# Sigmoid attention and a ReGLU layer in one kernel: a third unit of seven products in batch 2, whole chunks between the units, bursts of five and three

## The chip, the cores and the metric

One core of one Trainium2 chip runs the whole kernel in one launch. The time is the device time of one execution in microseconds. The engines are TensorE (PE; PEld is its weight load), VectorE (DVE), ScalarE (ACT), GpSimd (POOL) and SyncE (SP). POOL issues the loads, SP the DMA transposes and most stores.

## What is computed

```python
# q, k, v: (8 batches, 12 heads, 448 tokens, 64), float32
scores = q @ k.T / sqrt(64) - log(448)
attn = sigmoid(scores)
x = (attn @ v)  # heads side by side: 3584 tokens x 768
gate = maximum(x @ w_gate, 0)      # w_gate, w_val: 768 x 1536
val = x @ w_val
out = (gate * val) @ w_out         # w_out: 1536 x 768
```

## The kernel before

The kernel works in float16 with sums in float32 and goes over the batches 0 to 7. In each batch, scores are made in 21 *score units* (`qk_unit`): three groups `g` of four heads, seven query chunks `c` each; the order is g = 0 for units 0 to 6, g = 1 for 7 to 13, g = 2 for 14 to 20. A unit fills two PSUM banks and ScalarE takes the sigmoid of both into a tile PT. When a group's seven units are done, `pv` multiplies PT with v into two banks, and VectorE copies them, scaled, into `xT` (line 184). `pv` of a batch's last group (`pv_finish`) comes in the first burst of the next batch.

Scores come in *bursts* (`burst`), and between two bursts PE does work of the feed-forward layer of earlier batches. The order is written by hand: `cuts` splits the 21 units, `pv_at` puts the `pv`, `mix`, `hooks` and `given` say what goes between the bursts of batch 1, and `work` is the queue from batch 2 on. Within a burst the engines follow the order in which the program was written; each engine runs its own instructions strictly in that order.

The layer's 1536 columns are twelve *chunks* of 128. There are three forms of the work on them. A plain chunk (`gv`) is two products of six matmuls, a relu on ScalarE or VectorE, and a multiplication on VectorE into `hT`. For batch 0 chunks are done for 256 and 192 tokens apart (`HALVES`, `push_first`), in batch 1's mix. For batch 1, eight of twelve chunks are done as two *units of seven products* (`gv_split`, kind "s" in `work`): a seven-product block scheme, with four chunks and half the tokens at a time, that needs sums of weights (`gate_sums`, which overwrites part of `wv`, and S2, S1, S4 of `unit_sum_steps`) and of tokens (`split_sums`: T1, T2, T4, T3). The four other chunks of batch 1 are plain ("u"). From batches 2 and 3 on, pairs of batches use units "w" (`gv_pair`). The output is made in pairs of token tiles (`down_pair`, kind "y"), also with seven products; it needs sums of `wo` (`weight_sums(0..3)`, tiles T) and of `hT` (`token_sum_steps`). A pair in `SUMS_LATE` takes its products in another order, in which those that need no sums come first. In odd batches from 3 on, a burst lies inside a pair (`inner`, `amid`).

Within a unit or a pair, `ahead` is written before its first product, and `jobs` (`beside`) after the first few.

The eight PSUM banks are handed out in turn (`bank`, `later`), so a matmul that starts in a bank waits until the bank's last reader is done. SBUF tiles are shared in the same way by their tags.

From batch 2 on, q and k are turned around by `dma_transposes(b, g)`: two copies re-lay k and q of the group into a tile `rel` (VectorE, line 222), and one DMA transpose, issued by SP (line 226), writes `qkT`, which the group's score units read. `hold(b, g)` (line 857) is a copy on POOL that reads a `qkT`, so that the loads behind it on POOL's queue wait for the transpose. Batches 0 and 1 are transposed by PE.

The loads on POOL's queue are, in order: batch 0, weights w_gate and w_val in pieces, batch 1 between them, k and q of batch 2; then the hold for (2, 1), v of batch 2, batch 3, `wo`, and v of batch 3. The tiles of k and q of batches 0, 2, 3 and so on are one buffer, so a batch's load waits for the re-laying copies of the batch before.

Of the kernel before, what the change touches and what calls it, by code (L numbers as in the profile page):

```python
# [18 lines left out]
def kernel(  # L19
# [39 lines left out]
    gsbp = ctx.enter_context(tc.tile_pool(name="gsbp", bufs=6))  # L59
    first_sbuf = ExitStack()  # L60
# [34 lines left out]
    def tiles_of(b):  # L95
        if b not in in_tiles:
            pool = early if b == 1 else inp
# [59 lines left out]
    load_gv(6, 9)  # L157
    load_v(1)
    load(1, 2, 3, "kq")
    load_gv(9, 12)  # L160
# [57 lines left out]
    def dma_transposes(b, g):  # L218
        k16, q16, _ = in_tiles[b]
        rel = relp.tile([P, TW, P], FP16, tag="rel", name="rel")  # L220
        for ti, t16 in enumerate((k16, q16)):
            nc.vector.tensor_copy(  # L222
# [5 lines left out]
        )  # L228

# [136 lines left out]
    def open_late():  # L366
# [5 lines left out]
        late["X"] = pool.tile([P, 3, HD, S], FP16, tag="X", name="X")  # L372
        late["sums"] = ctx.enter_context(tc.tile_pool(name="sums", bufs=2))

# [28 lines left out]
    SUMS_LATE = {(1, 0), (1, 1), (2, 0), (2, 1), (3, NPP)}  # L403
# [152 lines left out]
    def early_sum_steps(j, f):  # L556
        views = []
        for i in range(3 * j, 3 * j + 3):
            t = early.tile([P, 2, 512], FP16, tag=f"PT{i}", name="S")
            flat = t[:].rearrange("p a y -> p (a y)")[:, 0 : HD * 2 * P]  # L560
            views.append(flat.rearrange("p (x y) -> p x y", y=2 * P))
# [15 lines left out]
    def batch_blocks(g, ks):  # L577
        x1, x2 = xT_tiles[2 * g], xT_tiles[2 * g + 1]
        lo, hi = slice(*ks), slice(HD + ks[0], HD + ks[1])
        return [late["X"][:, i, lo] for i in range(3)] + [x1[:, lo], x1[:, hi], x2[:, lo], x2[:, hi]]  # L580
# [13 lines left out]
    def gv_pair(g, f, beside, first_copy):  # L594
        x1, x2 = xT_tiles[2 * g], xT_tiles[2 * g + 1]
        T1, T2, T4 = (late["X"][:, i] for i in range(3))
# [77 lines left out]
    def split_sums(b):  # L674
        tile_ = xTp.tile([P, NPAIR, S], FP16, tag="xT", name="X2")
# [7 lines left out]
        sub(T1, B12, B11)  # L683
        sub(T2, B22, T1)
        sub(T4, B21, T2)
        sub(T3, B22, B12)
# [169 lines left out]
    def hold(b, g):  # L856
        nc.gpsimd.tensor_copy(gate[0:1, :], qkT_tiles[(b, g)][0:1, 0, 0:2])
# [40 lines left out]
    def next_work(jobs=(), alone=False, amid=None, ahead=()):  # L898
# [11 lines left out]
        if kind == "y":  # L910
            down_pair(g, i, beside, prepare, not work, scaled_act if alone else scaled, amid)
# [12 lines left out]
    for b in range(1, B):  # L924
        if b == 1:
            cuts, pv_at = (0, 3, 6, 9, 13, 17, 21), {3: (0, 2), 5: (1, 2)}
        else:
            cuts, pv_at = (0, 4, 7, 11, 14, 18, 21), {0: (-1, 2), 2: (0, 2), 4: (1, 2)}
# [8 lines left out]
        if b == 1:  # L937
            mix = (4, 3, 3, 3, 3, 4)
            hooks = {
                1: [(3, lambda: both(1, 1))],  # L940
                3: [(3, lambda: both(1, 2))],
                4: [(2, lambda: dma_transposes(2, 0)), (0, lambda: dma_transposes(2, 1))],
                5: [(4, late_loads)],
            }
            steps = itertools.chain.from_iterable(early_sum_steps(j, 2 * j) for j in range(4))
            given = ((0, 0, 1, 1, 1), (0, 1, 1, 1), (0, 1, 1, 1), (0, 1, 1, 0), (2, 0, 0, 0), (0, 1, 1, 1, 0))
# [15 lines left out]

        for m in range(count):
# [4 lines left out]
            if b == 2 and m == 3:  # L968
                jobs += [lambda: dma_transposes(3, 0), lambda: dma_transposes(3, 1)]
            elif b == 3 and m == count - 1:  # L970
# [6 lines left out]
            if b == 1:  # L977
                if m == 0:
                    load(2, 0, 1, "kq")
                    load(2, 1, 2, "kq")  # L980
                    load(2, 2, 3, "kq")
            elif m == (2 if b == 4 else 0) and b + 1 < B:
# [3 lines left out]
            if b == 2 and m == 0:  # L986
# [69 lines left out]
```

## Time and profile before

| | |
|---|---|
| median of 3 runs | 388.48 us (388.12 to 389.19) |
| the profiled execution | 389.02 us |
| its span, first to last instruction | 387.2 us |
| granted clock of TensorE, mean | 0.998 |
| batch 1's bursts and what lies between | 29.00 to 61.29 us |
| batch 2's | 61.29 to 95.79 us |
| the first output pair with its two bursts, in batch 3 | 95.79 to 105.73 us |
| issue of the transposes (2, 0), (2, 1), (2, 2) | 53.62, 56.10, 59.08 us |
| issue of the transposes (3, 0), (3, 1), (3, 2) | 82.64, 87.28, 96.04 us |
| POOL's hold passes | 60.16 us |
| v of batch 3, the last load behind it, landed | 92.16 us |

The times inside the execution are counted from the first instruction. Busy time of an engine is time in which it executes an instruction; a matmul's end is modelled, and matmuls that follow each other overlap in the table of groups. The time before a landing includes waiting in the queue.

### The profile page before, as it was taken

Reading aid. Unit: us, or ns where it says so; the run is one execution under the profiler, and the core shown is the slowest. Engines: PE = TensorE matmul, PEld = TensorE weight load, DVE = VectorE, ACT = ScalarE, POOL = GpSimd, SP = SyncE. Lnnn points to the kernel's source line nnn. Section 1 sums busy time; section 2 is a strip of 40 time slices with the busy share of each in tenths; the row PEclk is TensorE's granted clock in tenths of the full one; section 3 lists DMA queues with packets and bytes.
Section 4 is the critical chain, followed back from the end, with each engine's and each line's share of the span. In section 5 each row is a group of like instructions: output and inputs, shape, how many; then the busy total and the mean of one; then the engine's idle time right before and its main releaser. Section 6 shows DMA issues by size and latency. Waiting matters only on the chain.

```text
span 387.2 us, 8977 instructions
## 1 busy us (share of the span) xinstructions
PE 381.0 (98%) x3570; PEld 223.2 (58%) x3570; DVE 304.5 (79%) x609; ACT 227.3 (59%) x480; POOL 49.9 (13%) x73
## 2 busy tenths in 40 slices
PE   8999999999999999999999999999999999999995
PEld 6678776885555545555555554545455555555563
DVE  3455667769868999999868789999978788999563
ACT  5967887567777645555777764545477344333321
POOL 9543306100400003000300300000000000000000
PEclk9999999999999999999999999999999999999999
DMA  9999999999969303952599893222012220000335
GB/s 169 199 199 204 204 194 163 208 208 130 182 150 193 81 2 40 184 90 47 44 228 224 164 231 60 48 50 50 0 38 72 71 69 0 2 0 0 83 88 159
DMA packets 67421, 43.81 MB, mean 113 GB/s; under 512 B 35634, under 2 KB 64050, under 8 KB 67378
## 3 DMA queue, kind: packets, MB, share of 16 engines
q0 software_dynamic: 28960, 23.24, 39.3%
q1 hardware_dynamic: 37634, 19.24, 24.4%
q10 hardware_dynamic: 784, 0.75, 0.6%
q8 instruction: 28, 0.46, 0.5%
q14 instruction: 15, 0.12, 0.1%
HBM read 47.19 MB, written 11.01 MB: 150 GB/s over the span
## 4 chain that ended last, share of the span: by engine, by line
PE 97%; ACT 2%; DVE 0%; issue 0%
PE u L385 35%; PE g L385 16%; PE y L385 12%; PE qk_ps L239 10%; PE pv_ps L257 8%; PE g_ps L322 5%; PE v_ps L322 5%; PE u L708 2%; PE g L708 2%; ACT PT L187 2%; PE warm_ps L175 1%; PE trt L204 1%; ACT ysb L446 0%; DVE ysb L540 0%; DVE zeros L130 0%
## 5 line engine op out<-in xcount | busy, mean ns | idle before, releaser
L187 ACT ACTIVATE PT<-qk_ps 128x448 f16<-128x448 f32 (+3 forms) x318 | 150.9, 584 | 79.7 <-PE qk_ps L239 79.5
L385 PEld LDWEIGHTS <-S 128*128 128x128 f16 x576 | 56.4, 98 | 45.9
L624 DVE TENSOR_TENSOR gsb<-g,gsb 128x448 f32<-128x448 f32 x72 | 42.8, 624 | 8.0 <-PE g L385 7.7
L239 PE MATMUL qk_ps<-qkT 64*64 64x448 f16 (+2 forms) x756 | 47.5, 337 | 1.0 <-ACT ysb L446 0.6
L385 PEld LDWEIGHTS <-hT 128*128 128x128 f16 x318 | 29.5, 98 | 24.0 <-issue 6.1
L257 PE MATMUL pv_ps<-PT,v 64*64 64x448 f16 (+2 forms) x756 | 36.6, 329 | 0.0
L464 DVE SCALAR_TENSOR_TENSOR ysb<-y,ysb 128x384 f32<-128x384 f32 x33 | 18.4, 556 | 21.3 <-PE y L385 14.3
L184 DVE TENSOR_SCALAR xT<-pv_ps 128x448 f16<-128x448 f32 (+2 forms) x53 | 27.8, 567 | 8.2 <-PE pv_ps L257 7.1
L385 PEld LDWEIGHTS <-wg 128*128 128x128 f16 x216 | 20.1, 98 | 21.8 <-issue 4.3
L385 PEld LDWEIGHTS <-wv 128*128 128x128 f16 x216 | 21.1, 98 | 19.7
L446 ACT ACTIVATE ysb<-u 128x384 f32<-128x384 f32 x28 | 13.8, 491 | 30.6 <-PE u L385 26.5
L239 PEld LDWEIGHTS <-qkT 64*64 64x64 f16 x756 | 17.7, 106 | 21.3 <-issue 14.2
L385 PE MATMUL u<-wo,hT 128*128 128x384 f16 x156 | 29.8, 327 | 0.0
L111 POOL DMA_DIRECT2D k<-in_k_dram x14 | 10.9, 776 | 142.0 <-DVE rel L222 136.3
L257 PEld LDWEIGHTS <-v 64*64 64x64 f16 x756 | 21.4, 107 | 11.1 <-issue 0.5
L385 PE MATMUL u<-xT,wg 128*128 128x448 f16 x108 | 23.5, 354 | 0.0
L385 PE MATMUL u<-X,S 128*128 128x448 f16 x108 | 23.4, 352 | 0.0
L385 PE MATMUL g<-xT,wg 128*128 128x448 f16 x108 | 23.4, 352 | 0.0
L385 PE MATMUL u<-X,wv 128*128 128x448 f16 x108 | 23.4, 352 | 0.0
L385 PE MATMUL g<-X,S 128*128 128x448 f16 x108 | 23.4, 352 | 0.0
L385 PE MATMUL g<-xT,S 128*128 128x448 f16 x108 | 23.4, 352 | 0.0
L385 PE MATMUL u<-xT,wv 128*128 128x448 f16 x108 | 23.4, 352 | 0.0
(98 smaller groups left out, 563.1 us busy)
## 6 DMA issues: line engine op xcount, KB each, us to landing
out_dram<-ysb SPq DMA_DIRECT2D x50, 192.0 KB, 3.9
v<-in_v_dram POOLq DMA_DIRECT2D x8, 336.0 KB, 15.3
v<-in_v_dram POOLq DMA_DIRECT2D x16, 168.0 KB, 15.2
k<-in_k_dram POOLq DMA_DIRECT2D x4, 672.0 KB, 12.0
q<-in_q_dram POOLq DMA_DIRECT2D x4, 672.0 KB, 15.0
wo<-in_moe_w_out_dram POOLq DMA_DIRECT2D x2, 1152.0 KB, 19.2
k<-in_k_dram POOLq DMA_DIRECT2D x9, 224.0 KB, 12.1
q<-in_q_dram POOLq DMA_DIRECT2D x7, 224.0 KB, 12.4
```

The costliest lines, as they stand in the source:

```text
L111: nc.gpsimd.dma_start(t16[:, xs, cs], rows_of(src, b)[:, xs, cs])
L175: nc.tensor.matmul(ps[:, 0:n], zeros[:, 0:P], zeros[:, 0:n], start=True, stop=True)
L184: nc.vector.tensor_scalar(out=xT, in0=src, scalar1=XSCALE, scalar2=None, op0=AOP.mult)
L187: nc.scalar.activation(PT_ap, ps_ap, AF.Sigmoid, bias=sig_bias, scale=qk_scale)
L239: nc.tensor.matmul(out_of(hh)[o : o + 64, :], qkT[rows, c, cols], qkT[rows, NCH + c0 : NCH + c1, cols], start=True, stop=True, tile_positi ...
L257: nc.tensor.matmul(ps[hh][64 * r : 64 * r + 64, 0:qn], v16[rows, 2 * g + hh, c * D : (c + 1) * D], pieces[c][rows, hh, :], start=(c == 0), ...
L322: nc.tensor.matmul(ps[:, 0:qn], (wg, wv)[i][:, dc, f * P : (f + 1) * P], xT_tiles[b][:, dc, q0 : q0 + qn], start=(dc == 0), stop=(dc == ND ...
L385: nc.tensor.matmul(ps[:, 0:n], A[:, k_, :], W[:, k_, :], start=(first and k_ == 0), stop=(k_ == kn - 1), skip_group_check=True,)
L446: nc.scalar.activation(o, ps[:, 0:HM], AF.Copy, scale=OUT_SCALE)
L464: nc.vector.scalar_tensor_tensor(out=o, in0=ps[:, 0:HM], scalar=OUT_SCALE, in1=o, op0=AOP.mult, op1=AOP.add)
L624: nc.vector.tensor_tensor(out=gs[u][i][:], in0=ps[u][:, 0:S], in1=gs[u][i][:], op=AOP.add)
L708: nc.tensor.matmul(ps[j // 2][:, j % 2 * SQ : (j % 2 + 1) * SQ], sets[j][i][:, k_, :], W[:, k_, :], start=(first and j % 2 == 0 and k_ == ...
```

## The change

- **Batch 1's chunks 8 to 11** become a third unit of seven products, `("s", 1, 8)`. Its sums are put into output tiles (`output_views`), step by step beside batch 2's work.
- **Batch 0's chunks 10 and 11** leave batch 1's mix and come in batch 2 as plain chunks of all 448 tokens, `("u", 0, 10)` and `("u", 0, 11)`. Batch 1 has 16 pieces between its bursts and not 20. The queue of batch 2 is s0, u10, s4, u11, s8, where it was u8, s0, u9, s4, u10, u11.
- **Bursts in batch 2**: five, of 5, 3, 5, 3 and 5 units, where there were six of 4 and 3.
- **Relus** of six pieces of batch 0, not two, are on VectorE.
- **Re-laying copies**: those of (3, 0) and (3, 1) are on ScalarE, in the second and third unit of batch 2. (2, 1) and T1 are written ahead of batch 2's first burst, (2, 2) beside the first unit, (3, 2) last beside the first output pair of batch 3.
- **Loads**: v of batch 1 earlier; weight chunks 9, then 10 and 11, later; a hold for the transpose of (2, 0), and behind it k and q of (2, 1) and (2, 2), the weights' chunks 10 and 11 and v of batch 2. Behind the hold for (2, 1): batch 3, `wo`, v of batch 3. The loads of batch 4 wait for the copies of (3, 2), as before.
- **Output pair (0, 0)** is in `SUMS_LATE`, and its first copy is on ScalarE. `weight_sums(0)` is in the third unit, (1) to (3) at the first output pair, with VectorE's S2 ahead of it.
- **Memory**: k and q of batch 1 lie in a pool `mid` that stays; `split_sums` and the tiles X of batches 3 and later use it.

```diff
-    load_gv(6, 9)
     load_v(1)
+    load_gv(6, 9, (0,))
     load(1, 2, 3, "kq")
-    load_gv(9, 12)
+    load_gv(6, 9, (1,))
...
-    def dma_transposes(b, g):
+    def dma_transposes(b, g, copy=nc.vector.tensor_copy):
...
-    SUMS_LATE = {(1, 0), (1, 1), (2, 0), (2, 1), (3, NPP)}
+    SUMS_LATE = {(0, 0), (1, 0), (1, 1), (2, 0), (2, 1), (3, NPP)}
...
+    def output_views():
+        for _ in range(3):
+            t = ysbp.tile([P, 2, HD, 2 * P], FP16, tag="ysb", name="S")
+            yield t[:, 0]
+            yield t[:, 1]
...
-    push_first(1, range(0, 4))
-    for f0 in range(4, 12, 2):
+    push_first(1, range(0, 3))
+    push_first(1, (3,), False)
+    by_vector = {(1, 3), (0, 5), (0, 6), (1, 6), (1, 7), (0, 9)}
+    for f0 in range(4, 10, 2):
         for half in range(2):
             for f in range(f0, f0 + 2):
-                push_first(half, (f,), (half, f) not in ((0, 9), (1, 8)))
+                push_first(half, (f,), (half, f) not in by_vector)
...
+    def loads_behind_first():
+        dma_transposes(2, 0)
+        hold(qkT_tiles[(2, 0)])
+        load(2, 1, 2, "kq")
+        load(2, 2, 3, "kq")
+        load_gv(10, 12)
+        load_v(2)
+
     def late_loads():
-        dma_transposes(2, 2)
-        hold(2, 1)
-        load_v(2)
-        load(3, 0, NG, "kq")
+        hold(qkT_tiles[(2, 1)])
+        load(3, 0, 1, "kq")
+        load(3, 1, NG, "kq")
         load_o()
+        load_v(3)
...
-            work.extend([("u", 1, 8), ("s", 1, 0), ("u", 1, 9), ("s", 1, 4), ("u", 1, 10), ("u", 1, 11)])
+            work.extend([("s", 1, 0), ("u", 0, 10), ("s", 1, 4), ("u", 0, 11), ("s", 1, 8)])
...
-            cuts, pv_at = (0, 4, 7, 11, 14, 18, 21), {0: (-1, 2), 2: (0, 2), 4: (1, 2)}
+            cuts = (0, 5, 8, 13, 16, 21) if b == 2 else (0, 4, 7, 11, 14, 18, 21)
+            pv_at = {0: (-1, 2), 2: (0, 2), 4: (1, 2)}
...
-            mix = (4, 3, 3, 3, 3, 4)
+            mix = (3, 2, 3, 2, 3, 3)
...
+        if b == 2:
+            of_tokens = split_sums(1)
+            of_tokens[0]()
+            dma_transposes(2, 1)
...
+            if b == 2:
+                if m == 0:
+                    views = output_views()
+                    steps = itertools.chain.from_iterable(early_sum_steps(f, views) for f in (8, 10))
+                    some = lambda n: [lambda: next(steps)()] * n
+                    ahead.append(of_tokens[1])
+                    jobs += [lambda: dma_transposes(2, 2), late_loads, of_tokens[3], of_tokens[2], *some(1)]
+                elif m == 1:
+                    ahead += some(1)
+                    jobs += some(1)
+                elif m == 2:
+                    jobs += [*some(1), lambda: dma_transposes(3, 0, nc.scalar.copy)]
+                elif m == 3:
+                    jobs += some(3)
+                else:
+                    open_late()
+                    first_sums = token_sum_steps(0, 0)
+                    jobs += [
+                        *some(1), lambda: weight_sums(0), first_sums[0],
+                        lambda: dma_transposes(3, 1, nc.scalar.copy),
+                    ]
             elif b == 3 and m == 0:
-                jobs.append(lambda: (weight_sums(2), weight_sums(3)))
...
+                ahead += [first_sums[1], lambda: weight_sums(1)]
+                jobs += [*first_sums[2:], lambda: weight_sums(2), lambda: weight_sums(3)]
+                jobs.append(lambda: dma_transposes(3, 2))
```

More of the change, by code (lines that the diff above doesn't have):

```diff
@@ L228, in dma_transposes @@
         )
+        return rel
     def row_of(r, hh):
@@ L579, in batch_blocks @@
         lo, hi = slice(*ks), slice(HD + ks[0], HD + ks[1])
-        return [late["X"][:, i, lo] for i in range(3)] + [x1[:, lo], x1[:, hi], x2[:, lo], x2[:, hi]]
+        return [late["X"][i][:, lo] for i in range(3)] + [x1[:, lo], x1[:, hi], x2[:, lo], x2[:, hi]]
     def batch_sums_t1(g):
@@ L595, in gv_pair @@
         x1, x2 = xT_tiles[2 * g], xT_tiles[2 * g + 1]
-        T1, T2, T4 = (late["X"][:, i] for i in range(3))
+        T1, T2, T4 = late["X"]
         B11, B21, T3, B22 = x1[:, 0:HD], x1[:, HD:NDC], x2[:, 0:HD], x2[:, HD:NDC]
@@ L854, with hold @@
     open_banks("ring1")
-    def hold(b, g):
-        nc.gpsimd.tensor_copy(gate[0:1, :], qkT_tiles[(b, g)][0:1, 0, 0:2])
+    def hold(t):
+        nc.gpsimd.tensor_copy(gate[0:1, :], t[0:1, 0, 0:2])
     def both(b, g):
@@ L910, in next_work @@
         if kind == "y":
-            down_pair(g, i, beside, prepare, not work, scaled_act if alone else scaled, amid)
+            down_pair(g, i, beside, prepare, not work, scaled_act if alone or (g, i) == (0, 0) else scaled, amid)
         elif amid:
@@ L978 @@
                 if m == 0:
+                    load_gv(9, 10)
                     load(2, 0, 1, "kq")
[L980 to L982 removed]
+            elif b > 2 and m == (2 if b == 4 else 0) and b + 1 < B:
                 for g0, g1 in ((0, 1), (1, NG)) if b == 3 else ((0, NG),) if b > 3 else ():
```

60 lines of the change are left out of this document (27 added, 33 removed).

## The prediction, made before the changed kernel ran

> **What bounds the kernel now.** I read the page first: busy shares and the chain that ended last.
>
> ```profile
> PE 381.0 (98%) x3570; PEld 223.2 (58%) x3570; DVE 304.5 (79%) x609; ACT 227.3 (59%) x480; POOL 49.9 (13%) x73
> ...
> PE 97%; ACT 2%; DVE 0%; issue 0%
> ```
>
> TensorE (PE) is the bound from end to end. A change can take out only work that PE does, and every wait of PE that it makes is paid in full. Next the stretches that the change touches: batch 1, batch 2, and the first output pair in batch 3.
>
> ```profile
> 29.00:61.29 32.29, 32.29 (x441) 26.25 (x441) 21.66 (x53) 24.43 (x60) 8.53 (x12) 1.00 1.22 197
> 61.29:95.79 34.50, 34.50 (x385) 24.68 (x384) 26.39 (x49) 23.71 (x54) 6.70 (x10) 1.00 1.16 184
> 95.79:105.73 9.94, 9.94 (x100) 5.41 (x100) 7.79 (x13) 7.75 (x18) 4.96 (x7) 1.00 1.04 162
> ```
>
> After the stretch and its length come busy us of PE, weight loads, VectorE (DVE), ScalarE (ACT) and POOL. PE never idles there; VectorE and ScalarE are free a fifth to a third of the time. The timeline of PE gives the price of each piece of batch 2:
>
> ```profile
> 65.87 0.76 PE L239 MATMUL qk_ps<-qkT 64*64 64x448 f16 x12
> 66.56 1.32 PE L708 MATMUL u<-xT,wg 128*128 128x224 f16 x12
> ...
> 74.72 0.57 PE L239 MATMUL qk_ps<-qkT 64*64 64x448 f16 x8
> ...
> 76.92 1.31 PE L322 MATMUL g_ps<-xT,wg 128*128 128x448 f16 x6
> ...
> 79.30 0.76 PE L239 MATMUL qk_ps<-qkT 64*64 64x448 f16 x12
> ```
>
> From start to start: a burst of three score units 0.69 us, a unit of seven products (four chunks) 8.16, a burst of four with its `pv` 2.20, a plain chunk 2.38. Three bursts of 2.20, three of 0.69, two units and four chunks make 34.51, the window's 34.50. The changed order must keep this up, so I looked at what PE would wait for: ScalarE's sigmoids, VectorE's row of work in batch 3, and the DMA transposes, one alone and one beside loads.
>
> ```profile
> 61.71 3.60 ACT L187 ACTIVATE PT<-qk_ps 128x448 f16<-128x448 f32 x8 [0.48 <-PE qk_ps L239]
> ```
>
> ```profile
> 97.82 1.15 DVE L184 TENSOR_SCALAR xT<-pv_ps 128x448 f16<-128x448 f32 x2
> 99.19 0.56 DVE L441 TENSOR_SCALAR ysb<-u 128x384 f32<-128x384 f32 x1 [0.21 <-PE u L385]
> 99.66 1.35 DVE L376 TENSOR_TENSOR wo<-wo 128x2304 f16<-128x2304 f16 x1
> 100.93 1.35 DVE L376 TENSOR_TENSOR T<-wo,T 128x2304 f16<-128x2304 f16 x1
> 102.20 0.55 DVE L464 SCALAR_TENSOR_TENSOR ysb<-y,ysb 128x384 f32<-128x384 f32 x1
> ```
>
> The DMA view at 169 to 174 us, and at 150 to 163:
>
> ```profile
> qkT<-rel SPq DMA_TRANSPOSE x1, 4.0
> ```
>
> ```profile
> q0 software_dynamic: 1537, 1.35, 72.0%
> q1 hardware_dynamic: 1824, 0.46, 32.5%
> ...
> qkT<-rel SPq DMA_TRANSPOSE x1, 11.9
> ```
>
> Sigmoids start 0.43 us apart (eight in 3.60). A big weight difference takes VectorE 1.27 from start to start. A transpose lands 4.0 us after its issue when alone and 11.9 beside loads on POOL's queue (q0). Two more beside loads took 10.6 and 10.8; alone, 3.9 to 4.6.
>
> **The sum.** The profiled execution took 389.02 us (span 387.2, 1.8 around it), 0.5 above the median of 388.48. All terms are differences, so I set them on the median.
>
> **PE's own work.** Batch 2 gets three units, two whole chunks of batch 0 and five bursts: 3 x 8.16 + 2 x 2.38 + 3 x (2.20 + 0.19 for a fifth unit) + 2 x 0.69 = 37.79, 3.28 more. Batch 1 loses four pieces, two of 256 tokens (1.31 each) and two of 192 (0.99): 4.60 less. Together **-1.32**.
>
> **Bursts of five.** The fifth unit takes the banks of the second, whose last sigmoid ends 0.42 + 3 x 0.43 + 0.57 = 2.28 us after the burst starts; PE is there after 0.40 + 1.33 (`pv`) + 2 x 0.19 = 2.11. With the semaphore 0.2 each, three times: **+0.6** (0.3 to 0.7).
>
> **Copies ahead of `xT`.** Before batch 2's first burst VectorE now gets T1 and the re-laying copies of (2, 1), ahead of the two `xT` copies that free the banks of the first unit's first product. The k and q of (2, 1) are loaded only after POOL's hold on the transpose of (2, 0). In the trace the k and q of (2, 0) land at 51.5. Three chunk pairs were loaded before them (two loads of 576 KB, landing 6.04 us apart from the load before to the last); one pair is left, so 4.0 less, 47.5. VectorE gets there about then (batch 1's fifth burst starts near 46.7). Copies 0.7, transpose alone 4.0 to 4.6, POOL's gate copy 0.5: loads issued at 53. A first load of 224 KB landed 4.6 after its issue at 95.9 us, the next 1 to 2.5 later: 58 to 59.2, copies done at 58.3 to 59.5. Batch 2 starts at 61.29 - 4.60 = 56.7 and `xT` would start at 58.6. The banks are then free up to 0.9 late: **+0.4** (0 to 0.9).
>
> **The transpose of (2, 1).** Score unit 7, third of the second burst, needs it; before, it had 14 us to spare. Behind the hold, POOL now also queues (2, 2), the last 768 KB of weights and v of batch 2, about 9 us of loading at the 200 GB/s of the windows, so the transpose runs beside loads. From its issue PE needs 0.6 (first `xT` copy) + 8.16 + 0.40, about 9.2, to unit 7. With 10.6 to 11.9 PE waits 1.4 to 2.7: **+2.0** (0 with 4.0 to 6.7, as one that began with its loads at 96.0; 3.5 if weight loads are harder company). Measured company was k, q and v; the nearest rows are the three.
> By the Trainium skill ("DMA: Bandwidth & Descriptors", Queues, rings and completion order) each DMA engine takes turns between queues packet by packet. Taken strictly, with the rows' packets, the transpose's 1,824 packets wait for as many load packets; 1,350 of 0.52 KB and 474 of 0.88 KB are 1.1 MB, 5.7 us at 200 GB/s, which with its own 4.0 is an estimated 9.7: a wait of 0.5 and a sum of 391.4. The same rule gives about 10 for the row of 11.9, so the trace bears out the turns, and I keep the row.
>
> **Sums before the third unit.** After the last plain chunk VectorE does the gating product (which waits for a relu behind six sigmoids, until 3.6 us after the three-unit burst's start), then `gate_sums`, S2 and S1, each reading the one before (0.58): done at 5.9. Then the `xT` copy, done at 6.5; PE could start the unit at 0.69 + 2.38 + 2.6 = 5.7: **+0.8** (0.3 to 1).
>
> **Output pair (0, 0).** It now takes the late order, and beside it VectorE has S4, S3, two weight differences and the copies of (3, 2), all ahead of the `plus` that frees bank `y11`, which the third unit of the inner burst takes. From batch 3's first burst: `xT` copies done 3.0, S2 0.55, T2 1.27, S4 and S3 1.0, two differences 2.54, copies 0.6, `plus` 0.55: 9.5. PE: 2.20 + 5 products of 0.98 + 0.45 = 7.55. **+1.9** (1.6 to 2.2); in the trace the last `plus` here held no bank that this burst took.
>
> **Priced at nothing.** (3, 0) and (3, 1) copied by ScalarE: VectorE takes 0.39 for one, ScalarE's sigmoids of 768 to 1,024 columns 0.81 to 1.02, so 4 at most for four, beside the 4.3 us that ScalarE idles before a burst that follows a unit; if k of batch 3 lands late, the sigmoids behind wait as long. Transpose (3, 0), issued about 6.5 us into the second unit, has 1.7 + 3.07 + 2.6 + 8.16 = 15.5 us until batch 3, against 10.6 to 11.9; with `wo` as company perhaps 17.8: 0 to +2.6. (3, 2) and the loads of batch 4 start 9 us into batch 3, not at its start; at the 6.7 of the transpose at 96.0 it lands by 16, and unit 14 needs it at 22. Four more relus on VectorE fit (it is free 10 us in batch 1). One `plus` more and three `gate_sums` moved lie beside products.
>
> Sum: -1.32 + 0.6 + 0.4 + 2.0 + 0.8 + 1.9 = +4.4, so **392.9 us**; with the terms' bounds 390.9 to 395.
>
> **Rivals.**
> A, the other side: PE's stream stays closed and only its saved work shows, 388.48 - 1.32 = 387.2; with the fives' 0.6, 387.8. It needs VectorE ahead at `y11`: decided where its queue from batch 3's start is under 7.5 us instead of 9.5, and the transpose under 9.2. For: PE waits almost nowhere today and VectorE is free a fifth to a third of the time. Against: the order is fixed and the 1.27 rows are there. 0.2 in all, half under the 0.3% (1.2 us) that a measurement here can tell from no change.
> B, the transpose gets through in time (as the 6.7 row): 392.9 - 2.0 = 390.9. Against: three rows. 0.2.
> C, a long wait slows PE's clock. The windows show 1.00 and PE waits of 1.2 us at most, so no row shows it. If unit 7 waits over 3.4 us (+1.5) and a chunk of 2.38 then runs at half clock (+2.4): 396.8. By the Trainium skill ("TensorE: Matmul & The Clock Gate", Part 1) an idle window of about 3.4 us halves the clock; no run here shows it. 0.08.
> The forecast: 0.52. That the change doesn't do what it says is out: the products are counted in the order.
>
> Range 388.8 to 395.6: all of the forecast's, B, and A's upper part. Faster 0.1, within 0.3% 0.1, slower 0.8.
>
> **What would show it.** Windows: batch 1 near 27.7 long, batch 2 37.8 plus waits. Waits of PE: score line on the DMA of `qkT` 1.4 to 2.7 once; score line on VectorE's `plus` 1.6 to 2.2 once; the unit's first product on `xT` 0.4 and 0.8; three of 0.2 on sigmoids. DMA view: one transpose near 59 us landing after 10 us or more. The prediction is wrong if that one lands within 9 us, or if the `y11` wait is missing.

## The result: 400.96 us, 3.2% slower

| | before | after |
|---|---|---|
| median of 4 runs, us | 388.3 (388.01 to 389.19) | 400.96 (399.89 to 401.75) |
| ratio, 95% interval | | 1.032 (1.0291 to 1.035) |
| the profiled execution, its span | 389.02, 387.2 | 400.95, 399.2 |
| granted clock, mean | 0.998 | 0.995 |

The prediction was 392.9, with a range of 388.8 to 395.6. The sign was right and every wait that it had priced is there. What it had wrong is the size of three waits, for the transposes (2, 1), (3, 0) and (4, 0), the last two of which it had put at nothing; all three hang on the loads that run beside them. Times below are medians of runs, with lowest and highest; one run of `e11_alone_fours`, 1.5% above the fastest of its kernel, is left out of them.

First the profile page of the changed kernel: busy shares and the chain that ended last.

```profile
PE 382.5 (96%) x3582; PEld 226.0 (57%) x3582; DVE 312.4 (78%) x622; ACT 230.1 (58%) x478; POOL 52.6 (13%) x78
...
PE 83%; DMA 13%; ACT 2%; DVE 1%; issue 0%; POOL 0%; ACTq 0%; SPq 0%
```

DMA had no share in the chain before; now it has 13%. The windows of batch 1, batch 2 and the first output pair (columns as in the prediction: stretch, length, then busy us of PE, weight loads, VectorE, ScalarE, POOL, then clock, DMA share, GB/s):

```profile
28.73:56.44 27.71, 27.71 (x393) 22.07 (x393) 20.49 (x49) 21.91 (x52) 8.70 (x13) 1.00 1.03 154
56.44:104.14 47.70, 38.89 (x446) 31.01 (x445) 34.49 (x64) 29.37 (x60) 9.35 (x14) 1.00 1.19 171
104.14:116.93 12.79, 11.94 (x98) 6.03 (x98) 9.79 (x16) 7.79 (x17) 2.66 (x4) 0.87 0.21 39
```

Batch 1 is 27.71 long, as worked out (27.69). Batch 2 has 38.89 of work (37.79 and the 0.9 that the bursts of five add make 38.69) and 8.8 of waits. In the third stretch the clock is 0.87. Batch 1 also moved bytes at 154 GB/s where it had moved 197; the last sections come back to that. The timeline of PE, all lines of batches 2 to 4 with a wait over 0.15 us, and the line behind the fourth wait:

```profile
60.17 1.31 PE L723 MATMUL u<-xT,wg 128*128 128x224 f16 x12 [1.02 <-DVE xT L185]
72.54 0.38 PE L241 MATMUL qk_ps<-qkT 64*64 64x448 f16 x4 [3.67 <-DMA qkT<-rel]
92.52 1.31 PE L723 MATMUL u<-xT,wg 128*128 128x224 f16 x12 [0.71 <-DVE xT L185]
104.14 0.57 PE L241 MATMUL qk_ps<-qkT 64*64 64x448 f16 x8 [3.41 <-DMA qkT<-rel]
104.54 2.51 PE L259 MATMUL pv_ps<-PT,v 64*64 64x448 f16 x28
114.57 0.38 PE L241 MATMUL qk_ps<-qkT 64*64 64x448 f16 x3 [0.85 <-DVE ysb L469]
138.18 0.57 PE L241 MATMUL qk_ps<-qkT 64*64 64x448 f16 x8 [1.31 <-DMA qkT<-rel]
```

In order: `xT` before the first unit; the transpose of (2, 1) at unit 7; the sums before the third unit; the transpose of (3, 0) at batch 3's start; the bank `y11`; the transpose of (4, 0). The `pv` of 28 matmuls behind the fourth wait takes 2.51 where it takes 1.49 elsewhere: windows of 0.5 us show a granted clock of 0.87 from 104.5, 0.50 from 105.0 to 108.0 and 0.72 from 108.0, so about 3.4 us at one half, 1.7 lost.

The waits add to 10.97. To them come 0.9 for the fives (bursts of 2.71, 2.65 and 2.71 where 2.20 and a fifth unit's 0.19 make 2.39) and 1.7 for the clock; off go 1.32 of work and 0.55 for a wait that the old kernel had at 213.02 us. That is 11.7; the spans differ by 12.0.

Why the transposes were so late: the DMA view from 59.66 us, the issue of (2, 1), to 62.6; from 83.8 to 87, with (3, 0) issued at 83.87; and from 87 to 98 (packets, MB, share of the 16 engines; q0 has POOL's loads, q1 the transposes).

```profile
q0 software_dynamic: 990, 0.56, 136.0%
```

```profile
q0 software_dynamic: 458, 0.67, 116.8%
```

```profile
q0 software_dynamic: 1216, 1.73, 94.9%
q1 hardware_dynamic: 1104, 0.28, 22.9%
...
qkT<-rel SPq DMA_TRANSPOSE x1, 20.2
```

The first two answers have no line for q1: for over 3 us after its issue a transpose moves nothing, while loads that were queued before it move. The first packet of (2, 1) moved at 63.6, 4.0 us behind the issue, and that of (3, 0) at 87.6, 3.8 behind. Then the two queues go packet for packet, 1,216 of loads and 1,104 of the transpose, but 1.73 MB against 0.28. A transpose has 1,824 packets, so it is through when as many packets of loads have passed, or when the loads end. For (2, 1) it was the end: 1,197 packets of loads had passed when the last load landed at 71.75, and (2, 1) landed at 72.50. For (3, 0) both came together: 1,820 packets of loads passed between its first packet and its landing at 104.10, and the last load landed at 104.18.

### The profile page after: what moved, and what is told of

The parts are those of the page before. It is cut to its first block, busy times and chain, and to the rows that moved or that the text cites. A ratio compares the mean times of both kernels' runs of the same rounds, so it can differ in the third digit from the quotient of the medians.

```text
span 399.2 us, 9017 instructions
## 1 busy us (share of the span) xinstructions
PE 382.5 (96%) x3582; PEld 226.0 (57%) x3582; DVE 312.4 (78%) x622; ACT 230.1 (58%) x478; POOL 52.6 (13%) x78
## 4 chain that ended last, share of the span: by engine, by line
PE 83%; DMA 13%; ACT 2%; DVE 1%; issue 0%; POOL 0%; ACTq 0%; SPq 0%
PE u L390 32%; PE g L390 15%; DMA qkT<-rel 11%; PE y L390 11%; PE qk_ps L241 8%; PE pv_ps L259 7%; PE g_ps L324 3%; PE v_ps L324 2%; ACT PT L188 2%; DMA q<-in_q_dram 1%; PE trt L205 1%; PE warm_ps L176 1%; PE u L723 1%; ACT rel L223 0%; PE g L723 0%
## 5 line engine op out<-in xcount | busy, mean ns | idle before, releaser
L241 PE MATMUL qk_ps<-qkT 64*64 64x448 f16 (+2 forms) x756 | 48.8, 338 | 9.8 <-DMA qkT<-rel 8.4
L259 PE MATMUL pv_ps<-PT,v 64*64 64x448 f16 (+2 forms) x756 | 37.6, 335 | 0.0
L241 PEld LDWEIGHTS <-qkT 64*64 64x64 f16 x756 | 18.5, 106 | 31.5 <-issue 15.5
L390 PEld LDWEIGHTS <-wg 128*128 128x128 f16 x216 | 20.2, 98 | 21.8 <-issue 4.3
## 6 DMA issues: line engine op xcount, KB each, us to landing
v<-in_v_dram POOLq DMA_DIRECT2D x16, 168.0 KB, 15.5
k<-in_k_dram POOLq DMA_DIRECT2D x3, 672.0 KB, 11.9
```

Source lines behind the costliest of these rows:

```text
L241: nc.tensor.matmul(out_of(hh)[o : o + 64, :], qkT[rows, c, cols], qkT[rows, NCH + c0 : NCH + c1, cols], start=True, stop=True, tile_positi ...
L259: nc.tensor.matmul(ps[hh][64 * r : 64 * r + 64, 0:qn], v16[rows, 2 * g + hh, c * D : (c + 1) * D], pieces[c][rows, hh, :], start=(c == 0), ...
L390: nc.tensor.matmul(ps[:, 0:n], A[:, k_, :], W[:, k_, :], start=(first and k_ == 0), stop=(k_ == kn - 1), skip_group_check=True,)
```

## The experiments

The theory: PE waits because transposes share the DMA engines with loads that the change put beside them. A transpose waits for the loads queued before it and takes turns with those behind it, and has no duration of its own. Rivals: the transposes are slow by themselves (late copies, six in a shorter stretch); VectorE and ScalarE hold PE; the clock.

### Where the loads lie

**The company of (2, 1) taken away** (`e1_company_behind`).

```diff
 def loads_behind_first():
-    load_gv(10, 12)
-    load_v(2)
 def late_loads():
     hold(qkT_tiles[(2, 1)])
+    load_gv(10, 12)
+    load_v(2)
```

> The last 768 KB of weights and v of batch 2 are loaded behind the hold on (2, 1), no longer beside its transpose. Theory (the loads as company make the transpose of (2, 1) slow): it lands 4 to 7 us after its issue and not 12.8, PE's wait of 3.67 us at unit 7 goes, and the two loads are late in its place, by 2 to 3 us at the chunk that needs the weights or at the `pv` that needs v; batch 3's loads move later by as much, so the wait of 3.41 us for (3, 0) stays or grows by up to 2. Sum 398 to 403. Rival (the transpose is slow for another reason: its late start on its queue, the re-laying copies, its own packets): it still takes 10 us or more, the wait at unit 7 stays near 3.7 us and the two loads' lateness comes on top: 403 to 405.

398.84 us (ratio 1.0268, 1.0245 to 1.0291). The DMA view from 59 to 62 us, and PE's waits at 71 to 77:

```profile
qkT<-rel SPq DMA_TRANSPOSE x1, 6.1
```

```profile
71.08 1.62 PE L324 MATMUL g_ps<-xT,wg 128*128 128x448 f16 x6 [2.04 <-DMA wg<-in_moe_w_gate_dram]
73.39 2.26 PE L324 MATMUL v_ps<-xT,wv 128*128 128x448 f16 x6 [0.69 <-DMA wv<-in_moe_w_val_dram]
...
76.82 1.51 PE L259 MATMUL pv_ps<-PT,v 64*64 64x448 f16 x25 [0.43 <-DMA v<-in_v_dram]
```

The transpose took 6.1 us and not 12.8, and the wait at unit 7 is gone. The weights and v are late in its place, 3.16 together; at (3, 0) 1.68 was left. The company is the cause of the wait at unit 7, and the bytes are needed all the same.

**Loads ahead of the transposes** (`e2_loads_before`): k and q of (2, 1) and (2, 2) right behind (2, 0), no first hold, the second in batch 1.

```diff
+    def second_transpose():
+        dma_transposes(2, 1)
+        hold(qkT_tiles[(2, 1)])
+        load_gv(10, 12)
+        load_v(2)
...
+                5: [(2, second_transpose)],
...
                     load(2, 0, 1, "kq")
+                    load(2, 1, 2, "kq")
+                    load(2, 2, 3, "kq")
```

> k and q of (2, 1) and (2, 2) are loaded right behind (2, 0) without the first hold, the re-laying and the transpose of (2, 1) go into batch 1 ahead of its last burst's work, and the second hold stands there; everything else of the change stays. Theory (the two waits for transposes and the half clock come from where the loads lie): the waits of 1.02, 3.67 and 3.41 us and the 1.7 us at half clock go, the wait on y11 grows from 0.85 to 1.5 to 2.5 because PE is there sooner, and 1.31 at (4, 0) stays: 400.9 - 9.8 + 1 = 392, 390.5 to 393.5. Rival (the transposes are slow because batch 2 now issues six in a shorter stretch, whatever loads beside them): at least one wait of 3 us stays, 395 or more. Rival (the work on VectorE and ScalarE is what holds PE): the waits turn into waits on xT or the sigmoids, 397 or more.

397.59 us (1.0219, 1.0191 to 1.0247), a miss. The waits of 1.02, 3.67 and 3.41 are gone as expected, but weights and v came 1.49, 0.58 and 0.77 late, with the clock at one half from about 75 to 78.5. The first of them in PE's timeline:

```profile
70.99 1.31 PE L324 MATMUL v_ps<-xT,wv 128*128 128x448 f16 x6 [1.49 <-DMA wv<-in_moe_w_val_dram]
```

I had not asked who waits for the loads behind the hold.

**The weights ahead of the hold too** (`e5_weights_before`, here against `e2_loads_before`).

```diff
         hold(qkT_tiles[(2, 1)])
-        load_gv(10, 12)
         load_v(2)
...
                     load(2, 2, 3, "kq")
+                    load_gv(10, 12)
```

> As in the kernel whose loads of (2, 1) and (2, 2) come right behind (2, 0), and the weights' chunks 10 and 11 are loaded there too, ahead of the hold; behind the hold are only v of batch 2, batch 3, wo and v of batch 3, as in the kernel before. Theory (all that the transposes and late loads cost comes from loads that were put behind holds): PE has no wait on a DMA in batch 2, the clock stays at 1.00 there, and three waits are left: 0.71 before the third unit, 1.5 on y11, 1.33 at (4, 0). 388.5 - 1.32 + 0.9 (fives) + 3.5 = 391.6; 391 to 393. Rival (there is more to load in batch 2 than the queue can do, wherever it is put): a wait on a transpose or load of 2 us or more is left, and a half clock behind it, 394 to 398.

396.72 us (1.0242, 1.0195 to 1.029): the rival. The DMA view of 48 to 56 us and PE's wait:

```profile
qkT<-rel SPq DMA_TRANSPOSE x1, 11.0
```

```profile
59.73 0.57 PE L241 MATMUL qk_ps<-qkT 64*64 64x448 f16 x8 [2.77 <-DMA qkT<-rel]
```

Now (2, 0), 4.0 us in the changed kernel where it ran alone, took 11.0. It landed at 59.68; the last weights landed at 59.03. The waits of 0.70 and 1.48 are there as expected, and 1.66 at (3, 0).

**The old kernel without its hold** (`e7_old_no_hold`).

```diff
-        hold(2, 1)
```

> The kernel before without its one hold, so that v of batch 2, batch 3 and wo are loaded beside the transposes of (2, 1) and (2, 2). Theory (loads beside a transpose make it take 10 us or more, and it costs only what its due time does not cover): these two take 10 to 16 us and not 4.0, unit 7 is due 10.8 us after the issue of (2, 1) and unit 14 more than 19 after that of (2, 2), so PE waits at most 2 at unit 7; 388.5 to 390.5. Rival (the transposes of the changed kernel are slow because of the copies and issue there, not because of company): they keep to 4 to 5 us and the time stays within 0.3 of 388.5.

391.65 us (1.0088, 1.0071 to 1.0106). (2, 0) took 7.7 us, (2, 1) 5.8 and (2, 2) 11.7, against 4.6, 4.0 and 4.0 in the kernel before, so company slows transposes in the old order as well; of the two that I had put at 10 or more only (2, 2) got there. The 3 us came at a place that I had not named. VectorE's row:

```profile
61.35 0.39 DVE L222 COPY rel<-k 128x896 f16<-128x896 f16 x1 [3.92 <-DMA qkT<-rel]
```

There are two tiles `rel`. The copies of (2, 2) wait until the transpose of (2, 0) has read its own, and VectorE's row stands behind them for 3.92 us; PE then waits for products' banks, and the first chunk behind the burst starts at 65.78 where it had started at 63.49.

### The orders on VectorE

**Copies of (3, 2) earlier** (`e4_copies_first`).

```diff
+                jobs.append(lambda: dma_transposes(3, 2))
                 jobs += [*first_sums[2:], lambda: weight_sums(2), lambda: weight_sums(3)]
-                jobs.append(lambda: dma_transposes(3, 2))
```

> The re-laying copies of (3, 2) come ahead of S4, S3 and the two weight differences beside the first output pair. Theory (the loads of batch 4 wait for these copies, and the wait of 1.31 us for the transpose of (4, 0) follows from that): the loads start 3.0 to 3.5 us sooner and that wait goes; VectorE's row ahead of the last plus is as long as before, so the y11 wait stays at 0.85: 399.6, 399 to 400.2. Rival (the transpose of (4, 0) is late because of what it runs beside, not because of when its loads start): the wait stays over 0.8 and the time within 0.5 of 400.9.

399.76 us (1.0286, 1.0269 to 1.0303). Batch 4's first load was issued at 111.07, 3.2 sooner, and the wait at (4, 0) is gone, as the theory had it: issued at the same time (129.35 and now 129.61), (4, 0) took 6.3 us and not 8.8. The y11 wait was 1.48, not 0.85: in the changed kernel PE had come to it late, at half clock, and here the clock was 1.00 from 104 to 108.

**Three orders at once**, on top of `e5_weights_before` (`e6_all_three`).

```diff
-                jobs += [*first_sums[2:], lambda: weight_sums(2), lambda: weight_sums(3)]
-                jobs.append(lambda: dma_transposes(3, 2))
+                jobs += [*first_sums[2:], lambda: dma_transposes(3, 2)]
...
             plus(y1[:, lo], a)
+            if (g, p) == (0, 0):
+                weight_sums(2)
+                weight_sums(3)
...
-                    jobs += some(3)
+                    jobs += some(2)
...
+                    ahead += some(1)
```

> As the kernel with the weights ahead of the hold, and three orders on VectorE changed: the copies of (3, 2) right behind S4 and S3 of the first output pair, weight differences 2 and 3 behind the plus that frees y11, and S1 of the third unit behind the xT copy. Theory (the y11 wait is the two differences of 1.27 us ahead of the plus; the wait before the third unit is three sums ahead of the xT copy; the wait at (4, 0) is the copies of (3, 2) last in the row): all three waits go, PE's saved work of 1.32 less 0.9 for the fives is left: 388.1, 387.6 to 388.9. Rival (a wait that was hidden behind one of these comes out, of 1 us or more): 389.1 to 391.

394.57 us (1.0168, 1.0146 to 1.019), the best median of all variants of the changed kernel that load every byte, and not the 388.1. PE's waits:

```profile
59.34 0.57 PE L241 MATMUL qk_ps<-qkT 64*64 64x448 f16 x8 [2.61 <-DMA qkT<-rel]
...
100.74 0.57 PE L241 MATMUL qk_ps<-qkT 64*64 64x448 f16 x8 [2.64 <-DMA qkT<-rel]
...
110.62 1.14 PE L390 MATMUL y<-T,hT 128*128 128x384 f16 x6 [0.58 <-DVE ysb L469]
```

The third unit's wait and the one at (4, 0) are gone. In place of y11's 1.48 there are three shorter waits beside the same pair, 0.95 together (0.20, 0.58, 0.17). Both waits on transposes stay.

**The transposes alone** (`e9_alone`, then `e10_both_alone`), on top of `e6_all_three`: two more holds. The weights' chunks 10 and 11 move behind the first, `wo` and v of batch 3 behind the second.

```diff
         dma_transposes(2, 0)
+        hold(qkT_tiles[(2, 0)])
+        load_gv(10, 12)
...
                     jobs += [*some(1), lambda: dma_transposes(3, 0, nc.scalar.copy)]
+                    jobs += [lambda: hold(qkT_tiles[(3, 0)]), load_o, lambda: load_v(3)]
```

> As the kernel with the three orders changed, with two more holds: the weights' chunks 10 and 11 wait until the transpose of (2, 0) has landed, and wo and v of batch 3 wait until that of (3, 0) has. Theory (a transpose that runs alone takes 4 to 5 us, and the two waits left, 2.6 us for (2, 0) and 2.6 for (3, 0), are company): (2, 0) takes 6 at most and (3, 0) 5, both waits go, and 388.5 - 1.32 + 0.9 (fives) + 0.95 (what is left beside the first output pair) = 389.0; 388.4 to 390. Rival (loads that are held are late at their own users): wo comes 5 us later, a wait of 1 us or more shows at the third unit, at weight difference 1 or at the transpose of (3, 1), 390 to 393.

396.93 us (1.0189, 1.0165 to 1.0214): the rival in kind, and dearer than its 390 to 393. The DMA view from 84 to 89 us, VectorE's row, and PE's:

```profile
q1 hardware_dynamic: 1824, 0.46, 48.8%
...
qkT<-rel SPq DMA_TRANSPOSE x1, 3.9
```

```profile
97.67 1.36 DVE L381 TENSOR_TENSOR T<-wo 128x2304 f16<-128x2304 f16 x1 [2.79 <-DMA wo<-in_moe_w_out_dram]
```

```profile
73.04 0.38 PE L259 MATMUL pv_ps<-PT,v 64*64 64x448 f16 x2 [1.59 <-DMA v<-in_v_dram]
```

(3, 0) alone took 3.9 us, where it took 20.2 beside `wo`. And now v is late by 1.59 and 0.92 more, and `wo` holds VectorE for 2.79 and PE for 1.68 in the third unit. With (3, 1) held as well the price is higher:

> As the kernel with the two more holds, but the copies of (3, 1) are on ScalarE in the second unit too, right behind those of (3, 0), and wo and v of batch 3 wait for (3, 1). Theory: (3, 0) and (3, 1) both take 4 to 6 us, wo comes 2 to 3 us later still, and what (3, 1) loses beside loads in the kernel with (3, 0) alone goes; 388.4 to 389.5. Rival (wo is late at weight difference 0 or 1 and VectorE's row stands): a wait of 1 to 3 us in the third unit or the first output pair, 390 to 392.

401.26 us (1.0309, 1.0275 to 1.0342): VectorE stands 5.94 for `wo`, PE 4.83 behind it. Each of these orders of the same bytes leaves some user late.

**Bursts of four** (`e8_fours` on `e6_all_three`, `e11_alone_fours` on `e9_alone`).

```diff
-            cuts = (0, 5, 8, 13, 16, 21) if b == 2 else (0, 4, 7, 11, 14, 18, 21)
+            cuts = (0, 4, 8, 12, 16, 21) if b == 2 else (0, 4, 7, 11, 14, 18, 21)
```

> As the kernel with the three orders changed, with bursts of 4, 4, 4, 4 and 5 units in batch 2 and not 5, 3, 5, 3 and 5. Theory (a fifth unit waits about 0.3 for the second unit's banks, and a burst of four without a pv makes the chunk behind it wait for the first unit's banks): two waits of 0.3 go, two of about 0.5 come: 0.2 to 0.6 above the same kernel with fives. Rival (the chunk finds its banks free in time): 0.6 below it.

> As the kernel with the two more holds, with bursts of 4, 4, 4, 4 and 5. Theory (fives wait 0.3 each; a four without a pv makes the chunk or unit behind it wait about 0.5): within 0.6 above the same kernel with fives. Rival (a four costs nothing): 0.6 below it, at 388.4 or less.

396.13 (394.69 to 399.89) against 394.57, and 394.98 (393.35 to 396.95) against 396.93: the scatter between runs of one kernel is larger than the question. Inconclusive; answered below.

### The clock

Matmuls of no use inside the waits, in the changed kernel: ahead of batch 3 (`e3_warm`), and ahead of unit 7 too (`e12_warm_both`).

```diff
+                if (b, n, i) == (2, 1, 2) or (b, n, i) == (3, 0, 0):
+                    ps = bank("warm_ps")
+                    free.rotate(1)
+                    for _ in range(14 if b == 2 else 11):
+                        nc.tensor.matmul(ps[:, 0:S], wg[:, 0, 0:P], wg[:, 1, 0:S], start=True, stop=True)
                 qk_unit(b, g, c)
```

> Eleven matmuls of no use on weights already loaded are put ahead of batch 3's first burst (2 us of PE time inside the 3.41 us wait, their result is never read). Theory (the wait of 3.41 us left PE idle long enough for the clock to go to one half, which cost 1.7 us after it): the wait shrinks to 1.4, the granted clock stays at 1.0 at 104 to 108 us, and the kernel is 1.7 us less a y11 wait that grows by up to 1: 399.2 to 400.3. Rival (the half clock has another cause, such as load on the chip at that time): 400.9 within 0.4 and the half clock still in the records.

400.76 us (399.38 to 401.97): it could not tell. The wait at unit 7 was 4.22 this time, the clock halved there, and PE came to batch 3 too late to wait.

> The changed kernel with matmuls of no use at both long waits: fourteen ahead of unit 7 of batch 2 (2.7 us at 0.19 each, inside a wait of 3.7) and eleven ahead of batch 3's first burst (2.1 inside 3.4). Their result is never read. In the run with the second alone, the wait at unit 7 was 4.22 and the clock was at one half for 6.8 us behind it, so that it could not tell. Theory (PE's idle time is what halves the clock, 1.5 to 3 us each time): granted clock 1.0 in every run instead of 0.991 to 0.995, no half clock in the records of batches 2 and 3, the two waits short (1.0 to 1.5), a y11 wait of up to 1.9 because PE comes sooner, and 1.7 to 2.5 less in the median: 398.5 to 399.5. Rival (the clock halves whatever PE does there): half clock in the records, 400.5 or more.

400.07 us (398.94 to 401.31), half a miss. The profiled run, 401.25, still halved behind unit 7:

```profile
68.71 2.82 PE L990 MATMUL warm_ps<-wg 128*128 128x448 f16 x14
74.14 0.59 PE L241 MATMUL qk_ps<-qkT 64*64 64x448 f16 x4 [2.61 <-DMA qkT<-rel]
74.66 2.42 PE L324 MATMUL g_ps<-xT,wg 128*128 128x448 f16 x6
```

Six matmuls take 2.42 where they take 1.31. At batch 3 PE came too late to wait, and the clock is 1.00, so this run does not show what the wait there does to it. Three runs with a mean clock of 0.998 or more took 398.94, 399.37 and 400.07; two with 0.994 took 401.25 and 401.31. So some 2 us between runs of one kernel go with the clock. That idle time is what halves it was not shown: 2.61 us of it were left behind the useless matmuls at unit 7, and the clock halved.

### The bytes taken away

What was open: whether anything but the loads costs. Three kernels leave out the loads of `wo` and of the weights' chunks 10 and 11; POOL sets the tiles instead.

```diff
                     load(2, 2, 3, "kq")
-                    load_gv(10, 12)
+                    for wt in (wg, wv):
+                        nc.gpsimd.memset(wt[:, :, 10 * P : 12 * P], 0.01)
+                    nc.gpsimd.memset(wo[:], 0.01)
...
-        load_o()
```

> As the kernel with the three orders changed (394.57), but with 3.1 MB less to load: chunks 10 and 11 of both weights and all of w_out are left out and set to 0.01 by POOL in batch 1, so the output is not the layer's. All other work is as before. Theory (what is left against the kernel before is loads and transposes on the same DMA engines; PE's own terms are -1.32, +0.9 for the fives and +0.95 beside the first output pair): (2, 0), (2, 1) and (3, 0) land in 4 to 7 us, no wait on a DMA in batches 2 and 3, 389.0; 388.2 to 389.8. Rival (something on the engines themselves still costs): no DMA wait and yet 390.5 or more. Rival (the transposes are slow by themselves): waits of 2 us or more on qkT stay, 391 or more.

> The kernel before with the same loads left out and set to 0.01. Theory: its PE waits for no load, so that nothing changes, 388.5 within 0.5; the difference to the changed kernel with less loaded is then the change's own work on the engines, +0.5. Rival (setting the tiles on POOL holds something up in batch 1): 389 or more, and both kernels have that alike.

> As the changed kernel with less loaded, with bursts of 4, 4, 4, 4 and 5. With no loads in the way the price of a five can be read: theory (0.3 a five, two of three go, two fours without a pv make the chunk behind them wait about 0.5): 0 to 0.6 above the kernel with fives. Rival (a four costs nothing): 0.6 below, and at 388.4 level with the kernel before.

397.01, 389.95 and 398.78 us. No wait on a DMA is left in batches 2 and 3, but POOL's setting held VectorE in batch 1 (timeline of VectorE):

```profile
47.68 7.60 DVE L223 COPY rel<-k 128x896 f16<-128x896 f16 x1
```

That copy takes 0.39 elsewhere. It cost PE 4.89 in the new order and 0.68 in the old one, so the three could not answer. The same with the tiles set by VectorE in batch 0, in six pieces:

```diff
+    unloaded = [wt[:, :, 10 * P : 12 * P] for wt in (wg, wv)] + [wo[:, 3 * i : 3 * i + 3, :] for i in range(4)]
+    for at, t in zip(((1, 0), (1, 1), (1, 2), (1, 3), (2, 0), (2, 1)), unloaded):
+        after[at] = lambda f=after[at], s=set_to(t): (f(), s())
```

> As the changed kernel with less loaded, but the tiles left out are set to 0.01 by VectorE in batch 0, in six pieces, and not by POOL in batch 1, where the setting of 7.8 us held a copy of VectorE for 7.6 us and PE for 4.9. Theory (what is left against the kernel before is loads and transposes on the same DMA engines; PE's own terms are -1.32, +0.9 for the fives, +0.95 beside the first output pair): no wait on a DMA in batches 2 and 3, 389.0 and what the setting costs in batch 0 (0 to 1, the same in the kernel before with less loaded); 0 to 1.0 above that kernel. Rival (something on the engines still costs): no DMA wait and yet over 2 above it. Rival (the transposes are slow by themselves): waits of 2 us or more on qkT stay.

> The kernel before with the same loads left out, set by VectorE in batch 0 in six pieces. Theory: its PE waits for no load, so 388.5 plus what the setting costs, 388.5 to 389.5. Rival: it was held by loads that no wait shows, 388.0 or less.

> As the changed kernel with less loaded and the tiles set by VectorE, with bursts of 4, 4, 4, 4 and 5. With no loads in the way the price of a five can be read: theory (0.3 a five, two of three go; two fours without a pv make the chunk behind them wait 0.5): 0 to 0.6 above the kernel with fives. Rival (a four costs nothing): 0.6 below it.

399.27 (398.54 to 399.39), 399.5 (399.06 to 400.71) and 399.77 us (399.54 to 400.81). Setting the tiles costs some 10 us in batch 0, far more than I had thought, but alike: the first burst of batch 1 starts at 38.68, 39.22 and 39.28, where it starts at 29. From there on the windows can be compared. First the changed kernel, then the old one, from batch 1 to the end of the first output pair:

```profile
38.68:66.39 27.71, 27.71 (x393) 22.09 (x392) 20.48 (x50) 21.90 (x52) 2.60 (x4) 1.00 0.71 106
66.39:105.08 38.69, 38.57 (x445) 30.94 (x444) 32.05 (x60) 28.74 (x60) 7.18 (x11) 1.00 0.79 114
105.08:116.03 10.95, 10.16 (x99) 5.40 (x98) 10.78 (x19) 7.69 (x17) 4.16 (x6) 1.00 0.63 71
```

```profile
39.22:71.51 32.29, 32.29 (x441) 26.23 (x441) 21.96 (x53) 24.43 (x60) 4.93 (x8) 1.00 0.69 108
71.51:106.01 34.50, 34.50 (x385) 24.68 (x384) 26.35 (x49) 23.71 (x54) 4.79 (x7) 1.00 0.73 114
106.01:115.95 9.94, 9.94 (x100) 5.40 (x99) 7.79 (x13) 7.75 (x18) 4.94 (x7) 1.00 1.06 133
```

77.35 against 76.73: with the bytes out of the way the change costs 0.62, where PE's own terms (-1.32, 0.9, 0.95) make 0.53. The new order here has the early loads of `e5_weights_before` and the three orders of `e6_all_three`. Over the whole run the medians differ by 0.2 the other way; in the profiles the new order reaches batch 1 0.54 sooner. With fours, batch 2 is 39.32 long (66.99 to 106.31 us), 0.63 more than with fives: the fives were not the mistake.

## Why the prediction failed, step by step

| term | predicted | measured |
|---|---|---|
| PE's own work | -1.32 | -1.3 (batch 1 27.71; batch 2 38.69 with the fives, in `e16`) |
| bursts of five | 0.6 | 0.9 |
| copies ahead of `xT` | 0.4 | 1.02 |
| transpose (2, 1) | 2.0 | 3.67 |
| sums before the third unit | 0.8 | 0.71 |
| `y11` | 1.9 | 0.85; 1.48 where the clock stayed up |
| transpose (3, 0) | 0 | 3.41, and 1.7 of half clock |
| transpose (4, 0) | 0 | 1.31 |

- **The step that failed** is the duration of a transpose, "with 10.6 to 11.9", taken from rows as if it belonged to the transpose. The row of 11.9 began on an empty queue: issued at 150.97 with the first load at 150.90, its first packet moved at 152.2, 1.2 us later. (2, 1) was issued when loads had been queued since 52.53, and began 4.0 us late. From its first packet it took 8.9, where that row took 10.7. As far as these two rows go, the 1.7 by which the term was short lies in the late start and not in the turns.
- **(3, 0)** is the same step, priced at nothing because 15.5 us of cover stood against 10.6 to 11.9. It took 20.2. The row of 10.6 was this very transpose in the old kernel, issued at 82.64 with `wo` queued until 86.74 and v until 92.16, so "Measured company was k, q and v" does not hold for it. Its DMA view from 82.64 to 86.4 us has loads alone:

```profile
q0 software_dynamic: 633, 0.78, 118.6%
```

It too began 3.8 us late, and it landed at 93.28, 1.1 us behind the last load. What the row showed was when the loads ended. The hold in front of these loads, for (2, 1), in the old kernel and in the changed one:

```profile
60.16 0.48 POOL L857 COPY gate<-qkT 1x2 f16<-1x2 f16 x1 [15.70 <-DMA qkT<-rel]
```

```profile
72.62 0.18 POOL L874 COPY gate<-qkT 1x2 f16<-1x2 f16 x1 [13.60 <-DMA qkT<-rel]
```

It passed 12.5 us later, 8.8 of them because (2, 1) took 12.8 us and not 4.0. The last load landed 12.0 us later (92.16 and 104.18), and (3, 0) landed with it. So the slow (2, 1) is paid twice, at unit 7 and at batch 3.
- **The range** did not hold what the text had in it. The bounds written at the terms add to 389.4 to 395.5, not 390.9 to 395, and "with `wo` as company perhaps 17.8: 0 to +2.6" is in neither; with it the upper end is 398.1, still under 400.96. Both signs of being wrong looked for a shorter time, and neither came.
- **(4, 0)**: I checked the transpose of (3, 2), which had time, and not the loads of batch 4 behind its copies; they were issued at 114.27 and were the company of (4, 0). `e4_copies_first` shows it.
- **Rival C**, the clock, was given 0.08 and came, not at unit 7 but at batch 3. Its size was near (1.7 against 2.4), its condition was not.
- **Terms on VectorE's row** were right in place and near in size: 0.71 for 0.8, and 1.48 for 1.9. `e6_all_three` supports the rows named: with their orders changed the first wait is gone and the second is down to 0.95. The `xT` wait was 0.1 over its bound: q of (2, 1) landed at 59.16, the late end of what I had worked out, and batch 2 began at 56.44 and not at 56.7.
- **The packet rule** of the Trainium skill ("DMA: Bandwidth & Descriptors", Queues, rings and completion order), that a DMA engine takes turns between queues packet by packet, is borne out once a transpose has begun, with packets as the trace counts them: 1,216 and 1,104 from 87 to 98 us. With load packets of 1.4 KB (1.73 MB in 1,216) 1,824 turns let 2.6 MB of loads pass, 16.5 us at the 0.157 MB per us of those 11 us, and with 3.8 us of late start an estimated 20. That working was owed to (3, 0); I had made it for (2, 1) alone, with the small packets of other rows and no late start.

Why these loads ran in batch 2 at all: the new hold for (2, 0) kept POOL from issuing loads between 35.9 and 52.5 us, and the last load queued before it landed at 47.07. POOL's line, and windows of the changed kernel from 36 to 42 us and from 52 to 56.44 us:

```profile
52.30 0.18 POOL L874 COPY gate<-qkT 1x2 f16<-1x2 f16 x1 [16.42 <-DMA qkT<-rel]
```

```profile
36.00:42.00 6.00, 6.00 (x86) 4.54 (x87) 4.59 (x11) 4.60 (x12) 0.00 (x0) 1.00 1.35 201
52.00:56.44 4.44, 4.44 (x61) 3.57 (x54) 3.57 (x8) 3.52 (x9) 4.09 (x7) 1.00 0.61 78
```

The DMA engines moved 201 GB/s and then 78, where the old kernel, whose loads were queued ahead of its hold, moved 175 in the second stretch. So DMA time was left unused in batch 1 and was short in batch 2. Filling it is not enough by itself: `e5_weights_before` moved 198 GB/s over batch 1, and (2, 0) took 11.0 us beside the loads. In `e2_loads_before`, which loaded k and q of batch 2 early and left the weights behind a hold, the transposes were in time and the weights were late. Loads that are moved run beside a transpose or are late themselves (`e1`, `e2`, `e5`, `e9`, `e10`). `e16` against `e17` shows that without 3.1 MB of them, with the early loads and the three orders, what is left is PE's own 0.6. That no order of all the bytes could do better was not shown, only that the nine here did not.

## What to carry to other kernels

A transfer that shares its engines with queued loads has no duration of its own: price it by the loads queued before it, by turns with the packets of those behind it, and by when they end. Ask for each hold who waits for what stands behind it, whether the DMA engines run dry in front of it, and what is delayed behind it when it passes late. A change that shortens a stretch in which DMA is full moves the bytes' due times forward with it; count the bytes due by each point before counting the matmuls saved. The copies ahead of a slow transfer stand in an engine's row, so a wait there shows up somewhere else.

## What had not been expected of the hardware

- **The clock halves after less idle time than thought, and not always.** A wait of 3.67 us (changed kernel, unit 7) left it at 1.00, and so did two of 2.61 and 2.64 (`e6_all_three`); waits of 3.41, of 2.61 behind useless matmuls, and of 2.04 (`e1_company_behind`, clock 0.50 from 72.0 to 75.0) halved it. The stretch at one half was about 3.4 us, and 6.8 once (`e3_warm`). The Trainium skill ("TensorE: Matmul & The Clock Gate", Part 1) says that it halves after an idle window of about 3.4 us and that the windows run freely; the length of the stretches agrees, the whole window of idle time does not.
- **Setting a large tile on POOL held a copy of VectorE**: 7.60 us for one of 0.39, until POOL's instruction of 7.80 us ended (`e13_less_loaded`; in the old order, where the copy came later, 2.17). Subtractions of two operands that ran beside POOL's settings (at 45.83 and 47.21) kept their 0.55.
- **A transpose issued beside a full queue starts late**: packets came 1.2 us after the issue when alone (84.35, `e9_alone`) and 3.8 to 4.0 after it for (2, 1) and (3, 0), though the loads are on another queue. SP's own instruction lasted 6.05 and 7.44 us there and 1.51 when alone, so the delay may lie in the issue. The turns do not explain it; what does was not tested.
